# Weight loads, mask copies and rows: another order in the opening of a delta-rule attention and two expert layers

## The chip, the cores and the metric

One core of one Trainium2 chip runs the whole kernel. The metric is device time of one execution in microseconds (us); lower is better. A time given for a kernel is the median of three runs. The profile is of one further execution.

## The reference

```python
def _attn_ref(q, k, v, beta):            # (4, 8, 768, 48): batch, heads, steps, width
    k_n = k / (norm(k) + 1e-06)
    state = zeros((B, H, D, D))
    for t in range(S):
        y[:, :, t] = q_t @ state
        v_old = state^T k_t
        state = state + beta_t * outer(k_t, v_t - v_old)
def _moe_ref(x, w_in, w_out):            # 3072 tokens, 384 -> 2048 -> 384
    h = x @ w_in
    return (h * sigmoid(1.702 * h)) @ w_out
def _moe2_ref(x, domain_probs, w1, w2):  # 4 experts, 384 -> 1024 -> 384
    p = domain_probs / domain_probs.sum(-1)
    out = sum over e of p[:, e] * (relu(x @ w1[e]) @ w2[e])
```

The attention's output (heads side by side, 384 wide) goes into the first layer pair, and that into the four experts.

## The kernel before

**Attention.** The 768 steps are cut into 12 chunks of 64. In a chunk the recurrence becomes small matrix products: Gram products of the keys (`queue_g`), the inverse of a triangular matrix per head (`queue_first_inverse` for chunks 0 and 1 together, `queue_inverse` for later pairs), products of queries and keys that a causal mask weights (`queue_q`), and a chain (`queue_chain`): `ks`, `rest`, `solve`, `solved`, `cross`, `rest`, `solve`, `solved`, `read`, `write`, and the state's update. Chunk 1's chain needs chunk 0's state. In the inverse of the first pair TensorE makes two sets of 128 small products for chunk 0, `first` (L774) and `second` (L783), ScalarE copies between them, and VectorE merges the result (`out2`, L788).

**Weighting.** For each chunk `mask` (L496) reads the products of queries and keys from PSUM, multiplies them with the mask and writes them into the chunk's tile `pq`; four calls per chunk, all on VectorE.

**Expert layers.** They run on TensorE in three passes per product (the operands are split into a high and a low part). Tile 0 of the tokens (512 of them) is done in halves: the first half of its columns belongs to chunk 0, the second to chunk 1, and the first eight of the 16 weight blocks are done for the first half and then for the second. So the first layer starts as soon as chunk 0's rows `xs` exist (`take_x` on ScalarE or VectorE through L184, `take_rest` on VectorE, L949). Each block's products of layer one (L1108) are followed by those of layer two (L1215) for the block before, which need the gelu (L1230) and its split (L1232, L1233). Each product is a `tick`, between which chain steps of later chunks are emitted.

**Weight blocks.** `queue_w1(f)` brings block f (768 KB of 64-bit numbers) and makes 32-bit ones of them: `load` on SP's queue (L222), `small` (L293) and `low` (L296) on ScalarE, `shift` (L300, the combine) on VectorE, `hi` (L305) on ScalarE, `lo` (L308) on VectorE. For blocks 2 to 6, `touch` (L274) first takes the block's room and writes one column of it on VectorE: the load, which writes the same place, has to wait for that write, and so `touch` says when the load goes out. The load of block 7 waits for block 1's `lo`, and so on six blocks apart.

**Order.** A planner (`Order`, `Task`) walks through the program while it is being built. It has a clock for each engine and a cost for each task, and it emits the ready task with the lowest `prio`, and of equal ones the one made first. Each engine executes its instructions in the order of emission.

Of the kernel before, what the change touches and what calls it, by code (L numbers as in the profile page):

```python
# [12 lines left out]
ALU = mybir.AluOpType  # L13
# [4 lines left out]
C = 64  # L18
# [133 lines left out]
def delta_attention_moe_moe_kernel(  # L152
# [68 lines left out]
    def bulk(dst, src):  # L221
        nc.sync.dma_start(out=dst, in_=src)  # L222
# [29 lines left out]


    W, wdone, begun, turns, ended, marks = {}, {}, {}, {}, {}, []
    RAW = F1 - 6
    RING = [*range(RAW), *range(RAW + 2, F1), RAW, RAW + 1]

    def queue_w1(f, after):
# [12 lines left out]

        def touch():
            room()
            V.memset(cell["raw"][:, 0:1], 0.0)  # L274

        def load():
            if f in (0, F1 - 1):
                t = raw.rearrange("p h c -> p (h c)")
            else:
                if "raw" not in cell:  # L280
                    room()
                t = cell["raw"]
            dst = t.bitcast(I32) if wide else t
            bulk(dst if wide else dst[:, 0:768], w[f])
            if wide:
                pairs = dst.rearrange("p (n t) -> p n t", t=2)
                cell["lo"], cell["hi"] = pairs[:, :, 0], pairs[:, :, 1]
                cell["t"], cell["top"] = cell["lo"].bitcast(F32), cell["hi"].bitcast(F32)
            else:
                cell["t"] = t[:, 0:768]  # L290

        def small():
            nc.scalar.activation(out=cell["top"], in_=cell["top"], func=AF.Prelu, scale=2.0 ** -112, alpha=-2.0 ** 32)  # L293

        def low():
            nc.scalar.activation(out=cell["lo"].bitcast(U32), in_=cell["lo"].bitcast(U32), func=AF.Copy, scale=2.0 ** -29 * (1 - 2.0 ** -16),  # L296
                                 bias=7.5 * 2.0 ** -16 - 0.5)

        def shift():
            nc.vector.scalar_tensor_tensor(out=cell["lo"], in0=cell["hi"], scalar=3, in1=cell["lo"],  # L300
                                           op0=ALU.logical_shift_left, op1=ALU.bitwise_or)

        def hi():
            W[f] = wp.tile([128, 2, 768], F32R, name="w", tag=f"w{RING[f]}")
            nc.scalar.copy(out=W[f][:, 0, :], in_=cell["t"])  # L305
# [163 lines left out]
    def queue_q(u):  # L469
# [8 lines left out]
        lq = task(load, "HW", 1.9, (edone.get(u - 2), normed[u] if u > 1 else zeros[f"q{u}"]), lat=1.5, prio=p if u < 4 else p - 30, slack=5)  # L478
        ends, visits, masks = [], [], []
        whole = 2  # L480
        for o in range(2):
# [17 lines left out]
            visits.append(gram)  # L499
            masks += [(cell, lambda x=x, mask=mask: mask(x)) for x in range(2)]  # L500
            if len(visits) == whole:
# [6 lines left out]
                visits.clear()  # L508
                masks.clear()
        pdone[u] = task(lambda: None, None, 0.0, ends, lat=0.0, prio=p)  # L510

# [180 lines left out]
    def queue_first_inverse(us):  # L692
# [69 lines left out]
        for c, u in enumerate(us):  # L762
# [23 lines left out]
            def out2(u=u, c=c):  # L786
                t = Tb[u][:, :, H:]
                V.scalar_tensor_tensor(out=t, in0=cell["p", c][:, 1], scalar=hmask, in1=t,  # L788
                                       op0=ALU.mult, op1=ALU.add)

            n = NP // 2 if c else NP
# [24 lines left out]
    def queue_chain(u):  # L816
# [21 lines left out]
        ends, yev, halves = [], [], []  # L838
        whole = {}

        def y_free(hu):
# [142 lines left out]
        for hs in [halves[0:1], halves[1:2]] if u < 2 else [halves]:  # L984
# [46 lines left out]
            for h, y in zip(hs, reads):  # L1031
# [6 lines left out]
                else:  # L1038
                    ye = []
                    for kk in range(KD):  # L1040
                        a = task(lambda e, kk=kk, h=h: h["take_x"](e, kk), ("ACT", "DVE"), (0.3, 0.27), (y,), prio=-2)
                        ye += [a, task(lambda kk=kk, h=h: h["take_rest"](kk), "DVE", 0.28, (a,), prio=-2)]
                    xfree.setdefault((0, 0), []).append(y)
# [452 lines left out]
```

## Time and profile before

| | before |
|---|---|
| time, median of 3 runs | 1364.55 us (1362.36 to 1364.88) |
| the profiled execution | 1362.89 us |
| its span, first to last instruction | 1361.2 us |
| TensorE (PE) busy | 1329.9 us, 98% |
| VectorE (DVE), ScalarE (ACT), GpSimd (POOL) busy | 45%, 32%, 17% |
| granted clock of TensorE | 1.0 throughout (2.4 GHz) |

PE is TensorE's matmuls, PEld its weight loads. In a profile's row, `out<-in` are the program's tile names (`gp` products in PSUM, `pq` weighted products, `rw` and `raw` rooms of weight blocks, `su` the state with the solution, `ch` the chain's PSUM, `xs` the rows for layer one), L12 is line 12 of the kernel, and the bracket at a row's end gives the idle time of the engine before it and what ended it. Time counts from the start of the span.

### The profile page before, as it was taken

To read this page: it belongs to the slowest core of one execution; us is meant where nothing else is said; L and a number is where in the kernel's file an instruction comes from. 1 tells how busy PE (TensorE), PEld (TensorE's weight loads), DVE (VectorE), ACT (ScalarE), POOL (GpSimd) and SP (SyncE) were. 2 spreads that over 40 slices of the span, in tenths; PEclk is the share of its full clock that TensorE was granted. 3 is DMA by queue.
4 is the path that set the end of the run, shared out by engine and by line. 5 is a ranking of instruction groups with operands and counts; after the bars stand their busy time and mean duration, and the time that the engine had idled before them with its cause. 6 is when DMAs were issued, how large, how long until landed. Compare 5 with 4: busy or idle time off the path is not lost.

```text
span 1361.2 us, 28087 instructions
## 1 busy us (share of the span) xinstructions
PE 1329.9 (98%) x12304; PEld 1109.8 (82%) x12304; DVE 617.5 (45%) x1086; ACT 431.2 (32%) x827; POOL 226.0 (17%) x416
## 2 busy tenths in 40 slices
PE   5899999999999999999999999999999999999998
PEld 4788787778777888888888888888888888888887
DVE  7888674554745224233332234343233333234443
ACT  6874433543434334322222122222122221111111
POOL 4295848118381000000000000000000000000000
PEclk9999999999999999999999999999999999999999
DMA  7640313130111023001110000110000100011111
GB/s 234 216 139 14 92 38 87 52 75 2 40 52 40 5 89 111 9 8 33 42 32 20 0 20 31 38 37 8 0 32 32 31 20 8 1 31 32 31 31 47
DMA packets 36410, 63.29 MB, mean 46 GB/s; under 512 B 18688, under 2 KB 20160, under 8 KB 36288
## 3 DMA queue, kind: packets, MB, share of 16 engines
q1 hardware_dynamic: 36288, 61.50, 15.2%
q8 instruction: 96, 1.57, 0.5%
q14 instruction: 26, 0.21, 0.1%
HBM read 52.58 MB, written 7.91 MB: 44 GB/s over the span
## 4 chain that ended last, share of the span: by engine, by line
PE 89%; DVE 3%; POOL 3%; DMA 2%; issue 1%; SPq 1%; ACT 1%; DVEq 0%; POOLq 0%; ACTq 0%
PE ph L1108 41%; PE po L1344 24%; PE px L1215 13%; PE po L1375 5%; PE y L932 2%; POOL scr L665 1%; PE ch L896 1%; POOL itmp L663 1%; PE ch L881 1%; PE ch L915 1%; PE ch L955 1%; DMA rw<-in_w_dram 1%; DMA pq<-in_q_dram 1%; PE gp L491 1%; DMA kt<-in_kt_dram 0%
## 5 line engine op out<-in xcount | busy, mean ns | idle before, releaser
L1108 PE MATMUL ph<-xs,w 128*128 128x512 f32 (+1 forms) x2700 | 651.1, 383 | 0.8 <-ACT xs L184 0.5
L1108 PEld LDWEIGHTS ph<-xs,w 128*128 128x128 f32 x2700 | 491.2, 188 | 97.4 <-ACT xs L184 0.7
L1412 DVE SCALAR_TENSOR_TENSOR hh<-ph,hh 128x512 fp32r<-128x512 f32 x192 | 132.6, 691 | 502.0 <-ACT hh L1411 502.0
L1344 PE MATMUL po<-hh,w 128*128 128x512 f32 x1440 | 352.4, 389 | 0.0
L1344 PEld LDWEIGHTS po<-hh,w 128*128 128x128 f32 x1440 | 270.3, 188 | 56.2
L1411 ACT ACTIVATE hh<-ph 128x512 fp32r<-128x512 f32 x192 | 114.8, 598 | 615.3 <-PE ph L1108 615.3
L1215 PE MATMUL px<-gh,w 128*128 128x512 f32 (+1 forms) x972 | 228.6, 372 | 0.8 <-DVE gh L1233 0.8
L1215 PEld LDWEIGHTS px<-gh,w 128*128 128x128 f32 x972 | 167.5, 188 | 33.0 <-DVE gh L1233 2.1
L1233 DVE TENSOR_TENSOR gh<-ph,gh 128x512 fp32r<-128x512 f32 (+1 forms) x108 | 67.9, 630 | 130.2 <-ACT gh L1232 129.2
L1230 ACT ACTIVATE ph<-ph 128x512 f32<-128x512 f32 (+1 forms) x108 | 57.7, 535 | 188.3 <-PE ph L1108 181.8
L665 POOL TENSOR_TENSOR scr<-scr,itmp 128x30 f32<-128x30 f32 (+9 forms) x150 | 85.4, 569 | 11.8
L663 POOL TENSOR_TENSOR itmp<-scr 128x30 f32<-128x30 f32 (+9 forms) x150 | 78.4, 523 | 11.1
L1375 PE MATMUL po<-w,hh 128*128 128x384 f32 x384 | 72.3, 337 | 0.0
L1375 PEld LDWEIGHTS po<-w,hh 128*128 128x128 f32 x384 | 68.2, 188 | 2.7
L1232 ACT CAST gh<-ph 128x512 fp32r<-128x512 f32 (+1 forms) x108 | 58.3, 540 | 3.4
L184 ACT COPY su<-ch 32x192 f32<-32x192 f32 (+2 forms) x103 | 34.4, 334 | 37.0 <-PE ch L896 35.6
L1202 DVE TENSOR_TENSOR xs<-x,xs 128x512 fp32r<-128x512 f32 x72 | 45.3, 684 | 0.0
L833 POOL TENSOR_TENSOR v<-v,nr 128x192 f32<-128x192 f32 x40 | 21.2, 560 | 126.9 <-DMA v<-in_v_dram 74.5
L1201 ACT CAST xs<-x 128x512 fp32r<-128x512 f32 x72 | 39.7, 619 | 0.0
L888 DVE TENSOR_TENSOR v<-v,ch 128x384 f32<-128x384 f32 (+1 forms) x56 | 30.1, 551 | 18.6 <-issue 5.2
L250 DVE TENSOR_TENSOR w<-raw,w 128x768 fp32r<-128x768 f32 x32 | 30.7, 958 | 11.5 <-ACT w L249 10.7
L972 DVE TENSOR_TENSOR su<-su,ch 48x384 f32<-48x384 f32 x44 | 24.3, 552 | 24.4 <-PE ch L955 17.5
(134 smaller groups left out, 754.5 us busy)
## 6 DMA issues: line engine op xcount, KB each, us to landing
raw<-in_we_dram SPq DMA_DIRECT2D x32, 384.0 KB, 2.9
rw<-in_w_dram SPq DMA_DIRECT2D x14, 768.0 KB, 4.6
raw<-prd SPq DMA_DIRECT2D x20, 256.0 KB, 3.1
k<-in_k_dram SPq DMA_DIRECT2D x12, 384.0 KB, 4.8
kt<-in_kt_dram SPq DMA_DIRECT2D x24, 192.0 KB, 5.4
pq<-in_q_dram SPq DMA_DIRECT2D x24, 192.0 KB, 3.5
v<-in_v_dram SPq DMA_DIRECT2D x12, 384.0 KB, 3.4
out_dram<-oacc SPq DMA_DIRECT2D x80, 48.0 KB, 1.7
```

The costliest lines, as they stand in the source:

```text
L663: E.tensor_tensor(out=tv, in0=x[:, j:j + 1, j + 1:].broadcast_to([128, m, r]), in1=x[:, 0:m, j:j + 1].broadcast_to([128, m, r]), op=ALU.mult)
L665: E.tensor_tensor(out=x[:, 0:m, j + 1:], in0=x[:, 0:m, j + 1:], in1=tv, op=ALU.add)
L1108: mm(ps, lhsT=w[:, a, kk * 128:(kk + 1) * 128], rhs=xs[kk][:, b, cs], start=kk == 0 and i == 0, stop=kk == KD - 1 and i == 2)
L1202: nc.vector.tensor_tensor(out=s[:, 1, :], in0=src, in1=s[:, 0, :].bitcast(F32), op=ALU.subtract)
L1215: mm(px[d][:, cs], lhsT=w[:, a, 384 + d * 128:384 + (d + 1) * 128], rhs=gh[:, b, 0:cs.stop - cs.start], start=f == 0 and i == 0 and cs.sta ...
L1230: a = task(lambda: nc.scalar.activation(out=ph, in_=ph, func=AF.Gelu_apprx_sigmoid), "ACT", 0.05 + 0.43 * c, (pe,), **kw)
L1232: a = task(lambda: nc.scalar.copy(out=hi, in_=ph), "ACT", 0.05 + 0.43 * c, (a,), **kw)
L1233: a = task(lambda: nc.vector.tensor_tensor(out=lo, in0=ph, in1=hi.bitcast(F32), op=ALU.subtract), "DVE", 0.07 + 0.53 * c, (a,), **kw)
L1344: mm(po[kk], lhsT=w[:, a, 384 + kk * 128:384 + (kk + 1) * 128], rhs=hh[:, c, :], start=f == 0 and i == 0, stop=f == F2 - 1 and i == 2)
L1375: mm(ps, lhsT=hh[:, a, b * 128:(b + 1) * 128], rhs=w[:, c, 384:768], start=f == 0 and i == 0, stop=f == F2 - 1 and i == 2)
L1411: nc.scalar.activation(out=hh[:, 0, :], in_=ph, func=AF.Relu)
L1412: nc.vector.scalar_tensor_tensor(out=hh[:, 1, :], in0=ph, scalar=0.0, in1=hh[:, 0, :].bitcast(F32), op0=ALU.max, op1=ALU.subtract)
```

## The change

Nothing is computed otherwise; instructions are emitted at other places, by entries in a table `held_back` that a later step takes out and calls, and three weightings are cut in two.

- The touches of blocks 4, 5 and 6 are held back. Block 4's is emitted behind the second of chunk 0's four weightings, block 5's with its load behind chunk 0's merge (`out2`), block 6's behind block 0's combine.
- Of chunk 1's four weightings the first stays as it was. The other three become a plain copy on ScalarE out of PSUM (`raw_copy`), and a weighting in place on VectorE (`mask_there`), a new task that may run 6 us, by the planner's clock, after chunk 1's inverse is merged. The planner's costs of the four old tasks stay as they were.
- Block 5's `small` goes with its `low`; block 6's `low` goes in front of block 1's `hi`.
- Block 7's `small` and block 15's `shift` go behind the last of chunk 0's rows (`taken`).

```diff
@@ -251,6 +251,7 @@
         return t
 
 
+    held_back = {}
     W, wdone, begun, turns, ended, marks = {}, {}, {}, {}, {}, []
     RAW = F1 - 6
     RING = [*range(RAW), *range(RAW + 2, F1), RAW, RAW + 1]
@@ -269,9 +270,15 @@
         def room():
             cell["raw"] = wp.tile([128, 1536], F32, name="rw", tag=f"w{RAW + (f - 1) % 6}")
 
-        def touch():
+        def room_mark():
             room()
             V.memset(cell["raw"][:, 0:1], 0.0)
+
+        def touch():
+            if f in (4, 5, 6):
+                held_back["touch", f] = room_mark
+            else:
+                room_mark()
 
         def load():
             if f in (0, F1 - 1):
@@ -281,7 +288,10 @@
                     room()
                 t = cell["raw"]
             dst = t.bitcast(I32) if wide else t
-            bulk(dst if wide else dst[:, 0:768], w[f])
+            if f == 5:
+                held_back["load"] = lambda: bulk(dst, w[f])
+            else:
+                bulk(dst if wide else dst[:, 0:768], w[f])
             if wide:
                 pairs = dst.rearrange("p (n t) -> p n t", t=2)
                 cell["lo"], cell["hi"] = pairs[:, :, 0], pairs[:, :, 1]
@@ -290,17 +300,41 @@
                 cell["t"] = t[:, 0:768]
 
         def small():
+            if f in (5, 7):
+                held_back["small", f] = top
+            else:
+                top()
+
+        def top():
             nc.scalar.activation(out=cell["top"], in_=cell["top"], func=AF.Prelu, scale=2.0 ** -112, alpha=-2.0 ** 32)
 
         def low():
+            if f == 5:
+                held_back.pop(("small", 5))()
+            if f == 6:
+                held_back["low"] = bottom
+            else:
+                bottom()
+
+        def bottom():
             nc.scalar.activation(out=cell["lo"].bitcast(U32), in_=cell["lo"].bitcast(U32), func=AF.Copy, scale=2.0 ** -29 * (1 - 2.0 ** -16),
                                  bias=7.5 * 2.0 ** -16 - 0.5)
 
         def shift():
+            if f == F1 - 1:
+                held_back["shift"] = join
+            else:
+                join()
+                if ("touch", 6) in held_back and not f:
+                    held_back.pop(("touch", 6))()
+
+        def join():
             nc.vector.scalar_tensor_tensor(out=cell["lo"], in0=cell["hi"], scalar=3, in1=cell["lo"],
                                            op0=ALU.logical_shift_left, op1=ALU.bitwise_or)
 
         def hi():
+            if f == 1:
+                held_back.pop("low")()
             W[f] = wp.tile([128, 2, 768], F32R, name="w", tag=f"w{RING[f]}")
             nc.scalar.copy(out=W[f][:, 0, :], in_=cell["t"])
 
@@ -476,7 +510,7 @@
                 bulk(pq[DR[x]:DR[x] + D, x], q[u, x])
 
         lq = task(load, "HW", 1.9, (edone.get(u - 2), normed[u] if u > 1 else zeros[f"q{u}"]), lat=1.5, prio=p if u < 4 else p - 30, slack=5)
-        ends, visits, masks = [], [], []
+        ends, visits, masks, copies, later = [], [], [], [], []
         whole = 2
         for o in range(2):
             cell = {}
@@ -497,7 +531,30 @@
                                 in1=pmask[r:r + C, o].unsqueeze(1).broadcast_to([C, 8, C]), op=ALU.mult)
 
             visits.append(gram)
-            masks += [(cell, lambda x=x, mask=mask: mask(x)) for x in range(2)]
+            def raw_copy(x, o=o, cell=cell, flip=flip):
+                r, s = TR[x], half(x, flip)
+                nc.scalar.copy(out=pq[r:r + C, x, o::2, :], in_=cell["ps"][s:s + C])
+
+            def mask_there(x, o=o):
+                r, at = TR[x], pq[TR[x]:TR[x] + C, x, o::2, :]
+                V.tensor_tensor(out=at, in0=at, in1=pmask[r:r + C, o].unsqueeze(1).broadcast_to([C, 8, C]), op=ALU.mult)
+
+            def visit(x, n, mask=mask, raw_copy=raw_copy):
+                if u > 1 or n < (4, 1)[u]:
+                    mask(x)
+                    if not u and n == 1:
+                        held_back.pop(("touch", 4))()
+                    return
+                if n == 1:
+                    raw_copy(x)
+                if n == 2:
+                    raw_copy(x)
+                    copies[-1](1)
+
+            copies.append(raw_copy)
+            masks += [(cell, lambda x=x, n=2 * o + x, visit=visit: visit(x, n)) for x in range(2)]
+            if u == 1:
+                later += [lambda x=x, f=mask_there: f(x) for x in range(2)][1 - o:]
             if len(visits) == whole:
                 t = task(lambda fs=tuple(visits): weave(fs), "PE", 0.9 if u < 2 else 1.3,
                          (*placed[u], lq, begun[0], *(ends[-1:] if u > 1 else ())), prio=p + 1,
@@ -507,6 +564,7 @@
                     ends.append(c["end"][-1])
                 visits.clear()
                 masks.clear()
+        ends += [task(f, "DVE", 0.69, (ends[-1],), prio=p + 5, can=lambda: invdone[1].done + 6.0 if 1 in invdone and invdone[1].done is not None else None) for f in later]
         pdone[u] = task(lambda: None, None, 0.0, ends, lat=0.0, prio=p)
 
     def queue_beta(us):
@@ -787,6 +845,9 @@
                 t = Tb[u][:, :, H:]
                 V.scalar_tensor_tensor(out=t, in0=cell["p", c][:, 1], scalar=hmask, in1=t,
                                        op0=ALU.mult, op1=ALU.add)
+                if not u:
+                    held_back.pop(("touch", 5))()
+                    held_back.pop("load")()
 
             n = NP // 2 if c else NP
             parts = [slice(g, g + n) for g in range(0, NP, n)]
@@ -837,6 +898,12 @@
         lv = task(scale_v, ("POOL",) if u < 2 else ("POOL", "DVE"), (1.5,) if u < 2 else (1.9, 0.97), (lv, normed[u], ended.get(w)), prio=p + 1)
         ends, yev, halves = [], [], []
         whole = {}
+
+        def taken(h, kk):
+            h["take_rest"](kk)
+            if not u and h["hu"] and kk == KD - 1:
+                held_back.pop(("small", 7))()
+                held_back.pop("shift")()
 
         def y_free(hu):
             at = 0.0
@@ -1039,7 +1106,7 @@
                     ye = []
                     for kk in range(KD):
                         a = task(lambda e, kk=kk, h=h: h["take_x"](e, kk), ("ACT", "DVE"), (0.3, 0.27), (y,), prio=-2)
-                        ye += [a, task(lambda kk=kk, h=h: h["take_rest"](kk), "DVE", 0.28, (a,), prio=-2)]
+                        ye += [a, task(lambda kk=kk, h=h: taken(h, kk), "DVE", 0.28, (a,), prio=-2)]
                     xfree.setdefault((0, 0), []).append(y)
                     xfree.setdefault((0, 1), []).append(y)
                 h["cell"]["yev"] = ye
```

## Rows read from the trace of the kernel before

**Rows 1.** The page: engines' busy time, and one DMA queue (packets, MB, share).

```profile
PE 1329.9 (98%) x12304; PEld 1109.8 (82%) x12304; DVE 617.5 (45%) x1086; ACT 431.2 (32%) x827; POOL 226.0 (17%) x416
...
q8 instruction: 96, 1.57, 0.5%
```

**Rows 2.** Busy time by stretch: from:to, length, each engine's busy time (instructions).

```profile
0.00:55.00 55.00, 32.11 (x1155) 28.70 (x1156) 45.12 (x104) 37.99 (x75) 17.54 (x38) 1.00 0.73 228
```

**Rows 3.** The chain that ended last, 28 to 58 us: start, length, what.

```profile
34.05 2.11 issue
...
53.76 2.29 PE ph L1108 x17
```

**Rows 4.** Timeline of TensorE's matmuls, 30 to 38 us: start, length, instruction.

```profile
30.52 1.91 PE L774 MATMUL gp<-scr,scr 32*32 32x16 f32 x128 [3.05 <-DVE rw L274]
```

**Rows 5.** DMA, 28 to 33.85 us: queues (packets, MB, share), issues (us to landing).

```profile
q1 hardware_dynamic: 134, 0.75, 33.5%
...
rw<-in_w_dram SPq DMA_DIRECT2D x2, 768.0 KB, 4.4
```

**Rows 6.** DMA queues, 33.85 to 35 us.

```profile
q8 instruction: 1, 0.02, 5.1%
```

**Rows 7.** Timeline of SP's queue, three short stretches: loads of blocks 4, 5, 6.

```profile
30.43 0.33 SPq L222 DMA_DIRECT2D rw<-in_w_dram  x1
...
33.26 0.33 SPq L222 DMA_DIRECT2D rw<-in_w_dram  x1
...
37.87 0.33 SPq L222 DMA_DIRECT2D rw<-in_w_dram  x1
```

**Rows 8.** Timeline of VectorE, 0 to 72 and 72 to 135 us.

```profile
30.43 2.80 DVE L496 TENSOR_TENSOR pq<-gp,pmask 64x512 f32<-64x512 f32 x4
...
37.33 0.48 DVE L788 SCALAR_TENSOR_TENSOR scr<-gp,hmask,scr 128x256 f32<-128x256 f32 x1 [1.27 <-PE gp L783]
...
74.25 0.56 DVE L888 TENSOR_TENSOR v<-v,ch 128x384 f32<-128x384 f32 x1 [0.19 <-ACT su L184]
...
77.67 0.26 DVE L184 COPY stage<-su 128x192 f32<-128x192 f32 x1 [0.52 <-ACT su L184]
81.24 0.29 DVE L184 CAST xs<-y 128x128 fp32r<-128x128 f32 x1 [3.31 <-ACT xs L184]
...
122.51 1.71 DVE L888 TENSOR_TENSOR v<-v,ch 128x384 f32<-128x384 f32 x3 [0.46 <-PE ch L881]
```

**Rows 9.** Timeline of ScalarE, 0 to 72 us.

```profile
34.81 0.89 ACT L293 ACTIVATE rw<-rw 128x768 f32<-128x768 f32 x1 [1.95 <-DMA rw<-in_w_dram]
...
37.64 0.93 ACT L293 ACTIVATE rw<-rw 128x768 f32<-128x768 f32 x1 [1.17 <-DMA rw<-in_w_dram]
38.89 1.28 ACT L184 COPY su<-ch 32x192 f32<-32x192 f32 x4 [0.31 <-PE ch L896]
...
44.00 1.95 ACT L184 COPY su<-ch 64x384 f32<-64x384 f32 x4
...
52.00 0.91 ACT L293 ACTIVATE rw<-rw 128x768 f32<-128x768 f32 x1 [0.64 <-DMA rw<-in_w_dram]
52.81 0.57 ACT L184 CAST xs<-y 128x128 fp32r<-128x128 f32 x3
...
56.35 0.37 ACT L1230 ACTIVATE ph<-ph 128x256 f32<-128x256 f32 x1
```

**Rows 10.** Timeline of TensorE's matmuls, 55 to 112 and 112 to 136 us.

```profile
75.87 0.54 PE L896 MATMUL ch<-v,scr 32*32 32x48 f32 x32
...
79.10 0.34 PE L931 MATMUL y<-pq,stage 128*64 128x64 f32 x4
...
83.27 0.34 PE L931 MATMUL y<-pq,stage 128*64 128x64 f32 x4 [0.30 <-DVE xs L949]
...
95.43 1.22 PE L1215 MATMUL px<-gh,w 128*128 128x256 f32 x8 [0.78 <-DVE gh L1233]
...
124.43 0.80 PE L896 MATMUL ch<-v,scr 32*32 32x48 f32 x64
```

## The prediction, made before the kernel was run

> **What bounds the kernel now.** I read the page first, for the engines' shares, then the time in stretches, the chain that ended last, and at last the queues around the places where that chain stands still. The profiled execution took 1362.89 us with a span of 1361.2 us, so 1.7 us lie outside the span; the median of the three timed runs is 1364.55, 1.66 us above the profiled one. The sum below is made against 1362.89 and moved up by 1.66 at the end.
>
> TensorE is busy for 1329.9 of 1361.2 us [rows 1], so 31.3 us are all that any reordering can win. Of these, 55.00 - 32.11 = 22.9 us lie in the first 55 us [rows 2], before the first layer's products start in earnest at 53.76 [rows 3]; 8.4 us are left for the other 1306. The change touches only what is emitted between 28 and some 75 us, and behind 57 us TensorE has work in nearly every moment. It is worth what it moves the point from which TensorE runs full, less what it makes TensorE wait later.
>
> In the chain ahead of 53.76 one step is odd: 2.11 us of "issue" from 34.05, in the middle of the 128 products of L783 [rows 3]. No engine releases it. The queue q8 explains it: 96 packets with 1.57 MB, 16 KB each, while TensorE executes 2 x 12304 = 24608 instructions, which is 256 for one packet [rows 1]. So q8 carries TensorE's program, a block of 256 instructions (128 products with their weight loads) at a time. The stall comes after product 67 of L783, so the block before began 128 products earlier, at product 67 of the 128 in L774: 30.52 + 67/128 x 1.91 = 31.52 us [rows 4]. A fetch asked for then could have come at once; but no packet of q8 stands between 28 and 33.85 [rows 5], while 134 of the loads' move, and the one that comes starts behind 33.85 [rows 6], when block 4's load, issued at 30.43 [rows 7], has nearly drained. The fetch waited over 2.3 us behind a load issued 1.1 us before it. The Trainium skill, "DMA: Bandwidth & Descriptors", section "Queues, rings and completion order", says that a DMA engine takes turns between its queues, a whole packet of some 9 to 17 descriptors at a time. A load of 128 rows over 16 engines would be about one such packet, and then the two agree; a finer turn would speak against this change, since the load would then not make the fetch late, and the outcome would be rival (c) below, +1.0 in place of -0.2.
>
> **The fetch stall (load 4).** The write that opens block 4's room stood ahead of the first chunk's four weightings; it now stands behind two of them. The four take 2.80 us from 30.43 [rows 8], 0.70 each, so the load goes out at 30.43 + 1.40, about 31.9, some 0.4 us behind the request at 31.5. The stall then falls away whole: L783's end and the merge behind it come 2.11 us earlier. Bounds: nothing, if a request is later than I work out, and 2.11. I take 2.11 at this place.
>
> **The three copies on ScalarE.** One of the second chunk's four weightings stays on VectorE; three become copies of 64x512 on ScalarE. The nearest row has four copies of 64x384 out of PSUM in 1.95 us [rows 9], 0.49 each; with a third more columns at most 0.65. I take 0.6, three are 1.8 us (1.5 to 1.95). They stand where ScalarE waits 1.95 us for load 4 ahead of 34.81 [rows 9], from 32.86, so they end near 34.7 and cost nothing; without that cover it would be 1.8. VectorE saves 2.09 us there, but its next job is the merge at 37.33, for which it waited 1.27 us on TensorE [rows 8], so this is worth nothing until the stall is gone; then it is needed, since four weightings end at 36.06 and the merge can now start at 37.33 - 2.11 = 35.2.
>
> **What takes the stall's place.** Load 4, 1.45 us later, lands near 31.9 + 4.4 = 36.3 [rows 5], or 0.8 less without a fetch among it. Two activations of some 0.8 follow on ScalarE, so the first solve's copies, at 38.89 before [rows 9], come at about 37.6: 1.3 of the 2.11 are left. On SP's queue nothing stands between loads 4, 5 and 6, and what is behind them (block 15's load) waits for block 0's split in any case; so a load that waits there for its memset holds up the next weight load only. Load 5 moves from 33.26 to behind the merge, about 35.8, and load 6 from 37.87 to about 36.7 [rows 7]. Together they share the engines: loads 4 and 5 were first used at 34.81 and 37.64, 2.8 apart [rows 9], so 5 lands at 39.4 to 40.2 and 6 at 42.2 to 43.0, against 37.87 + 4.4 = 42.3 before. ScalarE's first activation of block 6 thus is no earlier than before. What helps is that the second one of block 6 (0.8 us) now stands behind the second solve's copies: they start at 43.0 to 43.85 instead of 44.00 [rows 9]. Of the 2.11 us some 0.15 to 1.0 arrive here; I take 0.6.
>
> **Rows ahead of two steps.** ScalarE waited 0.64 us for load 7 at 52.00, worked 0.8, and only then made the first layer's rows at 52.81 [rows 9]. With that step behind the rows, these come at about 51.1 to 51.4, and the first layer starts some 1.3 us earlier than 53.76. But it does not run on: its first gelu stood in ScalarE's queue at 56.35 [rows 9], behind block 7's two activations, three state copies and a weight cast. Their order changes, their sum doesn't, and load 7 can't land earlier: it waits for block 1's split, in front of which block 6's moved activation now stands, so it goes out within 0.3 us of before. What is saved is the 0.5 us of the rows themselves, up to 1.2 if loads 5 and 6 land early. TensorE needs that gelu for its second layer. Front: -0.4 to -1.2, and between 0 and -2.11 if my ScalarE chain is wrong; I take -0.6, nearer the small end, whose waits have rows. Block 15's combine, held back, leaves VectorE's queue ahead of the rows and comes right behind them, where VectorE waits for ScalarE; uncovered it would cost its length, by a weighting's 0.70 for 512 columns some 1.05 for its 768. The moved memsets write one column each and come at the place of others.
>
> **Three weightings near the second chunk's solve.** Same operation on the same size, 0.70 each: 2.1 us of VectorE. The planner lets them go 6 us behind the second chunk's merge on its own clock, with that chunk's chain's rank and a lower number, so ahead of its two subtractions, at 74.25 and behind [rows 8]. VectorE was done with the step before at 74.06; the first subtraction comes at 76.2, or 77.1 with a gating step between: 2.0 to 2.85 late. Behind it wait TensorE's solve and the readout. Slack: the solve at 75.87 came 1.06 us after the subtraction's end, and the readout at 79.10 [rows 10] 1.17 after the small copy's end at 77.93 [rows 8]; 2.2 together. So +0 to +0.6 and VectorE's idle 3.31 us ahead of 81.24 [rows 8] takes the rest. If no slack held, all 2.1 would show; if the 0.30 us stop at 83.27 [rows 10] falls away, -0.30. I take +0.4.
>
> The planner's clock then runs some 2 us later against the expert layers, so the third chunk's chain may be emitted earlier between them; its solve at 124.43 [rows 10] stands 0.3 us behind VectorE's three subtractions that begin at 122.51 [rows 8]. If it is emitted 2 us earlier TensorE waits there, up to 1.2; as no row shows the new order I take 0 and keep 0 to 1.2 for the range.
>
> **Sum.** -0.6 + 0.4 + 0 = -0.2: 1362.7 in the profiled execution's terms, 1364.3 as a median. The three runs of before spread over 2.5 us, so 0.2% (2.73 us) is about what can be told from no change.
>
> **Rivals.** (a) The front flows through: loads land early and ScalarE never waits. Then 2.11 us arrive, and the short stops at 83.27 (0.30) and ahead of 95.43 (0.78) [rows 10] go too, as VectorE has its splits done earlier: -3.2, 1361.3. For it speaks that ScalarE's waits ahead of 53 us (1.95, 1.17, 0.64) are all for loads; against it that the first two of these loads (4 and 5) go out later. Chance 0.19, three quarters of it beyond 0.2%. (b) Slower: the three weightings hit the second chunk's chain. From the point where the subtraction is over 2.2 us late, each further microsecond is TensorE's; with a 2.85 us delay, none of the slack and 1.2 us at the third chunk it is +4.0 - 0.6 = +3.4, 1367.9. For it speaks that VectorE stands idle for 0.19 us only ahead of 74.25; against it the 3.31 us ahead of 81.24 [rows 8]. Chance 0.12, most of it beyond 0.2%. (c) The change doesn't do what it says: the fetch is late for a reason of its own. Then the 2.11 stays and the merge is still at 37.3, so load 5 goes out at 37.9 and lands at 41.5 to 42.3, load 6 lands 2.8 later, at 44.3 to 45.1, and the second solve's copies behind block 6's first activation come 1.1 to 1.9 late; the rows give back 0.5: +1.0, 1365.5. Chance 0.09. The Trainium skill, "Runtime: NRT & Kernel Launch", section "Instruction fetch mechanics", calls the refill of a 16 KiB block mostly hidden; the 2.11 us row here disagrees, and by that rule the stall would be something else, as in (c). Chance of my own case 0.60.
>
> That gives 0.14 faster by over 0.2%, 0.76 within it, 0.10 slower. The range reaches from rival (a) most of the way to (b): 1361.2 to 1366.8.
>
> **What would show it.** No "issue" stall inside L783 and its last product near 35.1; copies of 64x512 on ScalarE ahead of 34.8; the first solve's copies near 37.6, the second's near 43.4; the rows near 51.3 and the first layer near 52.5, but the first gelu no earlier than about 55.7; TensorE waiting some 1 us ahead of its first second-layer product. VectorE's three in-place weightings near 74, and the readout of the second chunk within 1 us of 79.10. I am wrong if the first gelu comes at 54.5 or earlier, or if TensorE stands still for over 1 us between 75 and 90 or at 120 to 125.

## The result and the profile after

The changed kernel takes 1375.19 us (median of five runs, 1374.55 to 1378.27) against 1364.55 (1362.36 to 1367.41) in the same session: ratio 1.0090, interval 1.0078 to 1.0102. It is slower by 10.6 us between the medians and by 12.3 by the ratio, where I had forecast no change and given 0.10 to slower. The profiled execution is the median one, 1375.19 us, with a span of 1373.4.

The page first; the line answers to the first of [rows 1].

```profile
PE 1336.7 (97%) x12304; PEld 1115.3 (81%) x12304; DVE 615.5 (45%) x1083; ACT 433.1 (32%) x832; POOL 229.7 (17%) x420
```

TensorE executes the same 12304 products and is busy for 6.8 us more than before: some of them ran slower. Busy time by stretch says where (from:to, length, busy us with instructions of PE, PEld, DVE, ACT, POOL, then granted clock, DMA share, GB/s). Before:

```profile
55.00:75.00 20.00, 19.89 (x536) 17.86 (x539) 17.72 (x37) 15.90 (x30) 9.84 (x12) 1.00 0.69 227
75.00:100.00 25.00, 23.65 (x492) 21.91 (x480) 19.93 (x33) 18.85 (x39) 22.65 (x31) 1.00 0.40 118
100.00:140.00 40.00, 40.00 (x686) 33.36 (x687) 32.64 (x69) 18.14 (x40) 22.72 (x42) 1.00 0.06 19
140.00:190.00 50.00, 48.74 (x1002) 41.84 (x1002) 39.86 (x84) 20.99 (x54) 33.72 (x65) 1.00 0.26 73
```

After, with three shorter stretches cut out of them in the last lines:

```profile
55.00:75.00 20.00, 18.24 (x410) 16.70 (x409) 15.76 (x34) 13.40 (x25) 8.50 (x14) 0.92 0.74 231
75.00:100.00 25.00, 21.97 (x537) 19.33 (x540) 19.89 (x33) 17.99 (x35) 22.81 (x29) 0.86 0.44 139
100.00:140.00 40.00, 39.71 (x694) 34.41 (x687) 35.18 (x72) 19.88 (x44) 23.34 (x36) 1.00 0.04 12
140.00:190.00 50.00, 46.93 (x901) 38.60 (x899) 34.28 (x63) 20.69 (x52) 35.84 (x71) 0.97 0.31 78
...
71.78:78.61 6.83, 6.83 (x110) 5.85 (x110) 5.14 (x7) 1.76 (x5) 6.05 (x11) 0.50 0.44 156
...
92.26:95.67 3.41, 3.41 (x61) 2.95 (x58) 3.05 (x7) 2.31 (x6) 3.17 (x4) 0.50 0.37 94
...
184.42:187.83 3.41, 2.97 (x14) 2.97 (x15) 3.41 (x4) 0.00 (x0) 0.00 (x0) 0.50 0.00 0
```

Between 55 and 190 us TensorE stands idle for 8.1 us (135 less 126.9), before for 2.7 (135 less 132.3): 5.4 more. For 13.65 us in three stretches its clock is granted at 0.5, the lower level (1.2 GHz), where before it is at 1.0 from 50.7 us to the end of the span; that is worth up to 6.8 more, half of it in the stretch from 71.78, which stands behind a stop of 1.31 us at 70.24 that no engine released. With 0.9 that the opening is late, the sum is 13.1 us at most, and the last expert product comes 12.9 us later than before. So in this profile the loss is idle time, and the slow clock behind it.

The idle time in TensorE's timeline (start, length, instruction; in brackets the idle time ahead and what ended it). The readouts of the second chunk, L998, answer to L931 at 79.10 and 83.27 in [rows 10]:

```profile
70.24 0.60 PE L948 MATMUL ch<-su,kt 48*64 48x48 f32 x13 [1.31 <-issue]
...
81.23 1.24 PE L1282 MATMUL px<-gh,w 128*128 128x256 f32 x9
82.31 1.24 PE L1175 MATMUL ph<-xs,w 128*128 128x256 f32 x9
...
83.60 0.54 PE L963 MATMUL ch<-v,scr 32*32 32x48 f32 x32
...
85.10 0.86 PE L1282 MATMUL px<-gh,w 128*128 128x256 f32 x5
86.80 0.34 PE L998 MATMUL y<-pq,stage 128*64 128x64 f32 x4 [0.83 <-ACT stage L184]
...
91.44 0.34 PE L998 MATMUL y<-pq,stage 128*64 128x64 f32 x4 [2.16 <-DVE xs L1016]
...
184.86 2.08 PE L1282 MATMUL px<-gh,w 128*128 128x256 f32 x8 [2.33 <-DVE gh L1300]
```

TensorE's timeline before, with two rows of the first chunk's readouts and two of the second's:

```profile
49.99 0.48 PE L931 MATMUL y<-pq,stage 128*64 128x64 f32 x4
50.21 0.48 PE L932 MATMUL y<-pq,su 128*48 128x64 f32 x4
...
77.36 0.86 PE L1215 MATMUL px<-gh,w 128*128 128x256 f32 x5
78.06 1.11 PE L1108 MATMUL ph<-xs,w 128*128 128x256 f32 x8
...
79.60 0.34 PE L931 MATMUL y<-pq,stage 128*64 128x64 f32 x4
79.72 0.33 PE L932 MATMUL y<-pq,su 128*48 128x64 f32 x4
...
80.67 0.39 PE L1108 MATMUL ph<-xs,w 128*128 128x256 f32 x1
80.89 1.23 PE L1215 MATMUL px<-gh,w 128*128 128x256 f32 x9
```

The reader is to see what is missing after: in the kernel before, 13 expert products stand between the second chunk's last solve and its first readout (77.36 and 78.06), and 10 between the two readouts (80.67 and 80.89). In the changed kernel 5 and none do, and 18 more stand ahead of the solve (81.23 and 82.31). The order on TensorE is another one.

The same rows set right what the tables of the kernel before say of the clock. Its record begins at 50.7 us in that trace, and the 1.0 given for the time ahead of it is the absence of a record. There each row of four readouts follows the last by 0.22 us (49.99 to 50.21), later by 0.12 (79.60 to 79.72); in the profile after, where 0.5 is on record, it is 0.21 (92.48 to 92.69). So the opening ran at about half the pace, which fits the lower level.

The opening, in the rows that answer to [rows 4, 8, 9], from the timelines of TensorE, ScalarE and VectorE:

```profile
35.89 1.04 PE L841 MATMUL gp<-scr,scr 32*32 32x16 f32 x61 [0.47 <-issue]
...
54.65 2.28 PE L1175 MATMUL ph<-xs,w 128*128 128x256 f32 x17 [1.25 <-DVE xs L1016]
```

```profile
35.42 1.77 ACT L536 COPY pq<-gp 64x512 f32<-64x512 f32 x3 [1.19 <-DVE pq L530]
37.53 0.97 ACT L309 ACTIVATE rw<-rw 128x768 f32<-128x768 f32 x1 [0.33 <-DMA rw<-in_w_dram]
...
39.31 1.28 ACT L184 COPY su<-ch 32x192 f32<-32x192 f32 x4
...
44.83 1.96 ACT L184 COPY su<-ch 64x384 f32<-64x384 f32 x4
46.68 0.91 ACT L320 ACTIVATE rw<-rw 128x768 uint32<-128x768 uint32 x1
47.49 0.88 ACT L339 CAST w<-rw 128x768 fp32r<-128x768 f32 x1
...
52.22 0.60 ACT L184 CAST xs<-y 128x128 fp32r<-128x128 f32 x3
...
57.50 0.37 ACT L1297 ACTIVATE ph<-ph 128x256 f32<-128x256 f32 x1
...
86.39 0.60 ACT L184 COPY stage<-su 128x192 f32<-128x192 f32 x2
```

```profile
48.41 0.96 DVE L342 TENSOR_TENSOR w<-rw,w 128x768 fp32r<-128x768 f32 x1 [1.45 <-ACT w L339]
...
54.31 0.67 DVE L1016 TENSOR_TENSOR xs<-y,xs 128x128 fp32r<-128x128 f32 x3
...
77.80 2.65 DVE L540 TENSOR_TENSOR pq<-pq,pmask 64x512 f32<-64x512 f32 x3
```

The stall is down from 2.11 to 0.47, and the rows are out of ScalarE at 52.22 in place of 52.81. But VectorE's subtractions for these rows end later than before, so the first layer starts 0.9 us later, not 1.3 earlier. The first inverse's products, which the change doesn't touch, started 1.4 us later too (31.90 against 30.52).

### The profile page after: what moved, and what is told of

The parts are those of the page before. It is cut to its first block, busy times and chain, and to the rows that moved or that the text cites. A ratio compares the mean times of both kernels' runs of the same rounds, so it can differ in the third digit from the quotient of the medians.

```text
span 1373.4 us, 28100 instructions
## 1 busy us (share of the span) xinstructions
PE 1336.7 (97%) x12304; PEld 1115.3 (81%) x12304; DVE 615.5 (45%) x1083; ACT 433.1 (32%) x832; POOL 229.7 (17%) x420
## 4 chain that ended last, share of the span: by engine, by line
PE 93%; DVE 3%; DMA 1%; ACT 1%; issue 1%; SPq 0%; DVEq 0%; ACTq 0%
PE ph L1175 43%; PE po L1411 24%; PE px L1282 14%; PE po L1442 5%; PE y L999 2%; PE ch L963 1%; PE ch L948 1%; PE ch L1022 1%; PE gp L525 1%; DMA rw<-in_w_dram 1%; PE ch L982 1%; PE gp L612 1%; DVE scr L639 0%; DMA k<-in_k_dram 0%; ACT su L184 0%
## 5 line engine op out<-in xcount | busy, mean ns | idle before, releaser
L894 POOL TENSOR_TENSOR v<-v,nr 128x192 f32<-128x192 f32 x44 | 24.3, 584 | 118.8 <-DMA v<-in_v_dram 51.0
L184 DVE COPY su<-ch 32x192 f32<-32x192 f32 (+1 forms) x85 | 30.3, 356 | 17.4 <-PE ch L963 16.3
L530 DVE TENSOR_TENSOR pq<-gp,pmask 64x512 f32<-64x512 f32 x45 | 31.0, 689 | 10.7 <-PE gp L525 9.8
```

Source lines behind the costliest of these rows:

```text
L184: (nc.scalar.copy if e == "ACT" else nc.vector.tensor_copy)(out=out_, in_=in_)
```

## The experiments

Ratios are to the kernel before, run beside each on the same chip, with 95% intervals. I took the change apart into three: the held back touches (with load 5), the three weightings, and the order of ScalarE's and VectorE's steps for blocks 5, 6, 7 and 15.

**The kernel before, once more.** No edit. 

> The kernel before once more, for a second profile of it. In the profile of the changed kernel the second key load lands at 6.86 us in place of 5.39, ahead of anything the change touches. If that belongs to a single execution, this profile lies anywhere between the two, and the offset of the opening between profiles of one kernel is up to 1.4 us; if it belongs to the change, this profile agrees with the first one within 0.2 us at 28 us. Both theories expect a granted clock of 1.0 from 51 us on and a total of 1362 to 1366.

1363.98 us, clock 1.0 from 50.3 us on. The first inverse starts at 30.23 (30.52 in the first profile), which by itself would leave the late start to the change. The first expert product comes at 53.16 (53.10), the last one 1.3 us later than there. But over all profiles of this study the first inverse's products start anywhere from 29.8 to 32.5 us, with hardly a difference in the program ahead of them: at 30.00 and 30.50 in two versions that hold the touches back, at 32.16 in one that doesn't. So an opening that is a microsecond late in one profile proves nothing, and below only waits and medians are compared.

**The touches alone.** Of the change, only this is kept (and its calls):

```diff
+            if f in (4, 5, 6):
+                held_back["touch", f] = room_mark
...
+            if f == 5:
+                held_back["load"] = lambda: bulk(dst, w[f])
```

> Only the part with the held back touches of blocks 4, 5 and 6 (and load 5). Theory 1 (the three weightings in place ahead of the second chunk's subtractions starve TensorE near 75 and 86 us, and its clock then drops): this part is innocent, 1363 to 1366, clock 1.0 behind 51 us, the stall of 2.11 us inside the chunk's second inverse products gone or under 0.6. Theory 2 (the loads of blocks 4 to 11 are late, pile up with the q and kt loads at 60 to 66 us, so a fetch is late and TensorE stands still for 1.31 us near 69, and the clock then drops): if this part is what makes the loads late, 1368 to 1373, with a segment of granted clock 0.5 near 72.

1366.92 us, 1.0020 (1.0009 to 1.0032). The stall is 0.73 in place of 2.11, the clock is 1.0 from 55 us on, so theory 2's mechanism isn't there; and still it is slower, above theory 1's 1363 to 1366. ScalarE's timeline, and TensorE's:

```profile
42.36 0.88 ACT L306 ACTIVATE rw<-rw 128x768 f32<-128x768 f32 x1 [2.71 <-DMA rw<-in_w_dram]
43.24 1.27 ACT L184 COPY su<-ch 32x192 f32<-32x192 f32 x4
```

```profile
44.57 1.50 PE L968 MATMUL ch<-su,g 32*32 32x48 f32 x64 [4.91 <-ACT su L184]
```

Block 5's activation stands in ScalarE's queue ahead of the first solve's copies, and its load is now later: TensorE waits 4.91 us. Whether this wait makes the 0.0020 isn't shown: with ScalarE's steps reordered as well, the time is no better (1.0021, below).

**The weightings alone.**

```diff
-            masks += [(cell, lambda x=x, mask=mask: mask(x)) for x in range(2)]
+            masks += [(cell, lambda x=x, n=2 * o + x, visit=visit: visit(x, n)) for x in range(2)]
+            if u == 1:
+                later += [lambda x=x, f=mask_there: f(x) for x in range(2)][1 - o:]
...
+        ends += [task(f, "DVE", 0.69, (ends[-1],), prio=p + 5, can=...) for f in later]
```

> Only the three weightings: copied by ScalarE, weighted in place by VectorE behind the second chunk's merge. Theory 1: nearly the whole loss is here, 1371 to 1376, with TensorE's waits on VectorE at 86 to 92 us and granted clock 0.5 behind them. Theory 2: 1364 to 1368, the readout of the second chunk 2 to 3 us late but no segment of half clock.

1373.82 us, 1.0071 (1.0053 to 1.0090): most of the loss is here, with waits of 0.83 and 2.22 us ahead of the two readouts and 3.41 us of clock 0.5 from 87.1 and again from 124.6. Theory 1 holds as to the part. But TensorE's order differs from before in this run, and it is that of the whole change, while in the runs with the touches or the reordering alone it is that of before. So VectorE's time and the order were still mixed.

**The reordering alone.** Kept: `small` of 5 and 7, `low` of 6, `shift` of 15. 

> Only the order of ScalarE's and VectorE's steps for blocks 5, 6, 7 and 15 (block 6's second activation in front of block 1's first cast, block 7's first and block 15's combine behind the rows). Theory 1: 1363 to 1366, clock 1.0. Theory 2: block 7's load goes out 0.8 to 1.6 us later than before, the loads behind it too; where that makes a fetch late near 68 us, 1368 to 1373 with a segment of half clock, else within 2 us of before.

1365.25 us, 1.0004 (0.9994 to 1.0015): no change. The first layer started at 52.70 without a stop, as predicted for the whole, but a fetch stall of 0.73 us followed at 56, and the clock stood at 0.5 from 58.11 to 61.52; at 65 us this profile is 1.5 us behind.

**The weightings, tiny.** This tells VectorE's time from the order; seven of eight heads are left without their mask.

```diff
-                r, at = TR[x], pq[TR[x]:TR[x] + C, x, o::2, :]
+                r, at = TR[x], pq[TR[x]:TR[x] + C, x, o:o + 1, :]
```

> The weighting part alone, but each of the three weightings in place works on one head of eight (64 columns in place of 512), so two thirds of VectorE's 2.43 us at 74.77 or more go away; the other seven heads stay without their mask. The order of emission is that of the weighting part on every engine. There TensorE has 18 expert products more ahead of the second chunk's second solve than before, and none between the second chunk's two readouts. Theory O (the planner charges 0.69 for each weighting, so TensorE's order is another): the loss stays, 1370 to 1374, the readouts still wait without cover and the clock falls behind them. Theory V (VectorE's time ahead of the two subtractions): the loss goes, 1364 to 1367.

1371.97 us, 1.0060 (1.0045 to 1.0075). VectorE's three took 1.15 in place of 2.43 us (half, not the two thirds that I expected to go), and the loss stayed: the readouts wait 0.83 and 2.20 us.

**The weightings, without a price.** Now the order is that of before on TensorE, and VectorE does the full work at the same place.

```diff
-        ends += [task(f, "DVE", 0.69, (ends[-1],), prio=p + 5, can=...) for f in later]
+        ends += [task(f, "DVE", 0.0, (ends[-1],), prio=p + 5, can=...) for f in later]
```

> The weighting part alone, with the planner's price of the three weightings set to 0. TensorE's order is then that of the kernel before, instruction for instruction, while VectorE still does all 2.4 us ahead of the two subtractions. Theory O: most of the loss goes; TensorE waits about 1.1 us at the second chunk's second solve (2.2 late, less the 1.06 of cover), 1365 to 1368. Theory V: the loss stays, 1371 to 1375.

1365.00 us, 1.0014 (1.0004 to 1.0024). TensorE's timeline has the cover back, 13 products ahead of the first readout (the last 8 of them at 81.15) and 10 behind it:

```profile
78.96 0.54 PE L936 MATMUL ch<-v,scr 32*32 32x48 f32 x32 [0.84 <-DVE v L928]
...
81.15 1.12 PE L1148 MATMUL ph<-xs,w 128*128 128x256 f32 x8
82.20 0.34 PE L971 MATMUL y<-pq,stage 128*64 128x64 f32 x4
...
83.77 0.39 PE L1148 MATMUL ph<-xs,w 128*128 128x256 f32 x1
83.99 1.23 PE L1255 MATMUL px<-gh,w 128*128 128x256 f32 x9
...
86.45 0.34 PE L971 MATMUL y<-pq,stage 128*64 128x64 f32 x4 [0.38 <-DVE xs L989]
```

The weightings' own time (2.28 us here) costs 0.84 at the solve and little at the readout. Theory V is out.

**The whole change, without a price.** The same edit in the changed kernel. 

> The whole change with the same price of 0: every edit is there, TensorE's order is that of before. Theory O: 1365 to 1369, with no wait of over 1.5 us at the readouts. Theory V: 1372 to 1376, as the whole change.

1366.05 us, 1.0015 (1.0004 to 1.0025), clock 1.0 from 49.3 us on: one number in the planner takes back 0.0075 of the 0.0090.

**The change without the weightings.** Touches and reordering. 

> The change without the weighting part: the held back touches and ScalarE's order. Both theories: 1362 to 1366, since TensorE's order is that of before. The touches alone put the second activation of block 5 in front of the first solve's copies and the front was 4.0 us late; here it stands behind them, so the front (first expert product) should be at 52.0 to 53.5. If late loads are what matters (theory 2 of the first runs), a fetch stalls near 68 us and the clock falls: 1368 to 1372.

1366.55 us, 1.0021 (1.0012 to 1.0031), above the 1362 to 1366 that I expected. No fetch stalled near 68 us, so theory 2 missed again; but the profile has clock 0.5 from 60.41 to 63.82, and the first-layer run came at 54.77, 1.0 late, behind a first inverse as early as before (30.50). In ScalarE's timeline block 6's second activation stands ahead of block 1's cast, and VectorE's split of block 1, and behind it the rows, wait for that cast. The parts don't add up, either: this one costs 0.0021 and the weightings without a price 0.0014, but both together 0.0015. The next run moves the activation back.

**The cast first.**

```diff
         def hi():
-            if f == 1:
-                held_back.pop("low")()
             W[f] = wp.tile([128, 2, 768], F32R, name="w", tag=f"w{RING[f]}")
             nc.scalar.copy(out=W[f][:, 0, :], in_=cell["t"])
+            if f == 1:
+                held_back.pop("low")()
```

> The change without the weighting part, and block 6's second activation behind block 1's first cast in place of ahead of it. Theory R (the rows' subtractions stand on VectorE behind block 1's split, which waits for that cast): the split comes about 0.8 us earlier than the 48.88 of the run without the weighting part, the run of 17 first-layer products starts 0.5 to 0.8 earlier than its 54.77, and the time falls by as much, to 1365.5 to 1366.2. Theory L (loads 4 to 6 come too late for ScalarE, whatever its order): no change, 1366 to 1367.

1362.88 us, 0.9998 (0.9989 to 1.0007). From the instruction behind the second solve's copies to the split it takes 0.93 us (49.01 to 49.94) in place of 1.72 (47.16 to 48.88), which is theory R's 0.8. The run of 17 did not come earlier in this profile, whose opening was 1.9 us late from the start. The median moved by 3.7 us, out of the range of theory R and more than 0.8 explains; the rest may be the slow clock at 60 us, which this profile lacks, but one profile each doesn't show how often it comes.

**Block 6 behind the copies.** Both of block 6's activations behind that cast. 

> As the run before, and block 6's first activation, too, behind the second solve's copies and the cast. The copies stood behind it and so behind load 6, which landed at 44.36. Theory R and L both: the copies come at the end of the solve's first half, about 43.5 in place of 45.31, the split at 46.3 to 46.8; the 17 products at 52.6 to 53.4, so 0.4 to 1.2 before those of the kernel before (53.76); then 1362 to 1364 by either, if no fetch stalls and the clock holds. If the first expert products gain and the time does not, the gain is lost behind 55 us (the gelu of the first block, loads 8 to 11, a fetch).

1364.14 us, 0.9998 (0.9988 to 1.0009). Copies at 44.25, split at 47.16, first layer at 53.96: later than I expected, in a profile whose first inverse was 1.9 us late, and no gain in the median.

**The same in the whole change, without a price.** 

> The whole change with the price of 0, and block 6's two activations behind the copies and the cast: copies at about 43, the 17 products at 52.0 to 53.0, less 1.4 us of waits that the weightings cost at the second chunk's second solve and readout: 1362.5 to 1365.

1365.78 us, 1.0013 (1.0004 to 1.0023), above my 1362.5 to 1365. In this profile the opening was early and the first expert product came at 50.07, 3.0 us ahead of before; by 65 us only 0.3 were left, after 3.41 us of clock 0.5 from 57.11. The weightings then cost 1.1.

**The same without touches.** 

> ScalarE's order of the run with block 6 behind the copies, without the held back touches: the stall of 2.11 us stays and the first solve is as late as in the kernel before, but load 6 lands by 42.3. If the touches are worth anything, this is slower than the run with them; by the rows the copies come at 43.3 to 44.0, the 17 products at 52.3 to 53.0: 1362.5 to 1365.

1363.20 us, 1.0002 (0.9990 to 1.0015), with the 2.11 us stall in place. With block 6 behind the copies and the stall ended it was 1364.14 (0.9998); each of the two ratios is known to about 0.001, so whether ending that stall is worth anything up to 2 us can't be told from them.

**The order alone.** The kernel before with three tasks that issue nothing:

```diff
+        if u == 1:
+            ends += [task(lambda: None, "DVE", 0.69, (ends[-1],), prio=p + 5, can=...) for _ in range(3)]
         pdone[u] = task(lambda: None, None, 0.0, ends, lat=0.0, prio=p)
```

> The kernel before, with three empty tasks of 0.69 in the planner where the three weightings were put. They issue nothing: every instruction is that of before, all four weightings at their old place on VectorE, and only the order is that of the weighting part. Theory O (the order): 1369 to 1373, with no cover between the second chunk's two readouts, waits there of 0.8 and 2.2 us, and a wait of over 2 us for a gelu near 120. Theory V (VectorE's 2.4 us ahead of the subtractions): 1363 to 1366.

1372.36 us, 1.0073 (1.0049 to 1.0098): as slow as the weighting part, though the three tasks add no instruction. On TensorE the order is that of the whole change. But more than the order moved: the planner chooses between engines by the same clocks, and the page shows other counts on VectorE, ScalarE and GpSimd than [rows 1], so the expectation's "every instruction is that of before" doesn't hold for ten small copies and one scaling:

```profile
PE 1335.9 (97%) x12304; PEld 1115.6 (81%) x12304; DVE 615.7 (45%) x1083; ACT 431.6 (31%) x829; POOL 226.9 (17%) x420
```

TensorE's timeline:

```profile
77.45 1.24 PE L1217 MATMUL px<-gh,w 128*128 128x256 f32 x9
78.53 1.24 PE L1110 MATMUL ph<-xs,w 128*128 128x256 f32 x9
...
81.32 0.86 PE L1217 MATMUL px<-gh,w 128*128 128x256 f32 x5
83.01 0.34 PE L933 MATMUL y<-pq,stage 128*64 128x64 f32 x4 [0.83 <-ACT stage L184]
...
87.52 0.34 PE L933 MATMUL y<-pq,stage 128*64 128x64 f32 x4 [2.02 <-DVE xs L951]
...
183.13 1.21 PE L1217 MATMUL px<-gh,w 128*128 128x256 f32 x8 [2.33 <-DVE gh L1235]
```

The first half of tile 0 has 72 products of layer one and 63 of layer two; the next one needs the rows that these readouts make. The 135th starts at 81.90 here and at 81.84 before, but the 136th at 90.63 and 85.66. TensorE did the same work as early, and had nothing left for the readouts. Near 120 us the wait was 0.88, not the 2 that I expected, and this profile also has 6.83 us of clock 0.5 each from 54.72, ahead of all this, and from 88.85, and 3.41 from 184.43. At 183.13 a gelu's split waits in VectorE's queue; its timeline:

```profile
178.02 3.48 DVE L583 TENSOR_TENSOR scr<-gp,gmask 32x256 f32<-32x256 f32 x8 [0.65 <-PE gp L556]
...
182.65 0.76 DVE L1235 TENSOR_TENSOR gh<-ph,gh 128x256 fp32r<-128x256 f32 x2
```

That is 100 us downstream of the three tasks: the planner's clock had moved, and eight small weightings of a later chunk (178.02) now stand in front of the split, which the kernel before makes ahead of them.

**Both mends.** The change, price 0, cast first. 

> The whole change, with the price of 0 and block 6's second activation behind block 1's first cast. If these two are the causes, what is left of the loss is the 1.2 to 1.4 us that the weightings themselves cost at the second chunk's second solve and readout, less 0 to 1.0 from the opening: 1363.5 to 1365.5. If another part of the change costs, 1366 or more, as with the price alone.

1366.68 us, 1.0016 (1.0000 to 1.0032), which misses my 1363.5 to 1365.5: with the weightings in, the cast's place gave nothing back. By my own terms another part of the change still costs something, and which one stays open. Its profile has waits of 1.1 us at the second chunk's solve and 1.0 of issue near 69 us, and clock 1.0. No version is faster than the kernel before by more than the runs spread.

## Why the prediction was wrong

**The order on the planner's clock: the step that failed.** I wrote that the planner's clock "then runs some 2 us later against the expert layers", looked for the harm at the third chunk only, and, "as no row shows the new order", took 0 and kept 0 to 1.2. Measured, this term is about +10 us (1.0073 alone; 1.0090 against 1.0015 in the change). The planner holds the second solve back by three times 0.69 and fills TensorE with 18 expert products, 2.16 us of them by the rows at 77.45 to 79.61, in a stretch where they are finite. TensorE then waits for 0.83 and about 2.1 us at the readouts, and for 0.9 to 2.7 us once or twice where a gelu's split stands behind other work on VectorE; and behind most of these stops the clock fell. I had taken the expert products for an endless filler. The missing filler isn't all of it: with the price, ScalarE makes both `stage` copies (86.39, just ahead of the first readout), the first of which VectorE made at 77.67 in [rows 8], and VectorE does a scaling (88.44) and a weight block's `lo` (89.31) before the rows' subtractions (90.62) that the second one waits for. That the price does the harm is shown; how it divides between the filler and these steps, no run shows. The order could have been had before the prediction only by working the planner through.

**Three weightings near the second chunk's solve.** +0.4 predicted, with 2.2 us of slack counted as 1.06 at the solve and 1.17 at the readout. The first part was there: three weightings of 2.28 us leave a wait of 0.84. But I added the two slacks, and what the first didn't take, these 0.84 us, TensorE had lost before it came to the readout. At the readout 0.38 shows in place of the 0.30 of before; in all the expert products are 1.4 us later behind the readouts than ahead of the solve, and the median says 1.9 (1.0014). So the term is mis-sized by 1.0 to 1.5. Rival (b) named the right place, but its price, +3.4, was that of the delay, with 1.2 us for the order, at the third chunk.

**The fetch stall.** Nearly right at its place: 0.47 for 2.11, 0.73 with the touches alone, 2.10 and 1.42 with the other two parts, where they are not held back. So most of the stall went, not the whole of it. Had the fetch been late for its own reason, as in rival (c), it would have stayed. The rule of the Trainium skill, "DMA: Bandwidth & Descriptors", section "Queues, rings and completion order", that a DMA engine takes turns by packets agrees with that.

**Copies on ScalarE at no cost.** Right: 1.77 us for 1.8, and ScalarE waits for load 4 behind them (0.33). They started 1.19 us after ScalarE was free, since they wait for VectorE's weighting.

**What takes the stall's place.** Right for the first solve, not for the second. Without a price the first solve's copies come at 37.57 (37.6 predicted) in a profile that began 0.5 us early, and the second's at 44.47 (43.0 to 43.85 predicted, 44.00 before): ScalarE had waited 1.93 us for load 6, which went out at 36.85, near the 36.7 predicted, and was there at 43.57, not by 43.0. No row shows the 0.8 us that I took off for a load without a fetch among it.

**Rows ahead of two steps: -0.6.** Wrong in sign: touches and reordering without the weightings cost 2.9 us (1.0021), and with an opening as early as before their first layer came 1.0 us late. In the change ScalarE's half of the rows is 0.6 earlier, but TensorE needs VectorE's half. I followed ScalarE's queue and not VectorE's, in which block 1's split, 1.45 us idle behind the cast that block 6's activation had been put ahead of, delays everything to the rows. The reordering alone, with no load later, had the first layer at 52.70; its lead was gone by 65 us, as was that of the profile with the early opening. First gelu at 57.50, in the opening that was 1.4 us late; I had said not before 55.7.

My own sign for being wrong, TensorE standing still for over 1 us between 75 and 90, came true at the edge: the stop of 2.16 us began at 89.28. A plainer one did too: the second chunk's readout came at 86.80, not within 1 us of 79.10.

## What to carry over

A planner's cost is part of the program: a price on a moved step can reorder every engine behind it, and move steps between engines, so price the order apart from the work, with a task that issues nothing and with the work at price 0. Count a filler before leaning on it: here 135 products are all there is up to the second chunk's rows, and in the order that spends 18 of them early the loss was five times that of the wait they fill (0.0073 against 0.0014). When an engine's wait ends on two engines' results (ScalarE's rows, VectorE's rests), follow both queues. Look where a record begins before reading a level out of it.

## What the runs showed of the hardware

A stop of TensorE can cost twice. The clock, at 1.0 from 51 us, was granted at 0.5 for 6.83 us from 71.78, behind a stop of 1.31 us; for 3.41 from 92.26, behind stops of 0.83 and 2.16; for 3.41 from 184.42, behind one of 2.33. Not each stop is followed by a fall: the whole change without a price, with stops of 0.84, 0.38 and 0.95 (at 173.47), kept 1.0, both mends with 1.01 and 1.07 did, and the weighting part did behind 2.33 at 183.78. But each of the eleven falls that the profiles have between 65 and 1300 us stands behind a stop, also one each in two versions with the order of before: 3.41 us from 172.64 behind 1.22 (block 6 behind the copies) and from 174.75 behind 1.16 (the weightings without a price). Between 54 and 64 us it fell in four of the sixteen profiles, of programs that hardly differ there (the order alone and the kernel before, for one pair); that may be behind the 5 us and more by which runs of one kernel differ, which one profile of each can't show.

A fetch of TensorE's program can stop it again later: 1.31 us near 69 in the change, 0.72 at the same product with the weightings alone, 0.73 at 56 with the reordering alone. Each of these stops comes a whole number of blocks of 128 products, to within 2, behind the one inside the first inverse in the same profile: 512 products behind it near 56, 766 near 69. The Trainium skill, "Runtime: NRT & Kernel Launch", section "Instruction fetch mechanics", calls the refill mostly hidden; in these rows it is not.
